# State reads kept batch by batch, and their split moved forward in block 7 of a fused attention and feed-forward kernel

## The chip, the cores and the metric

The kernel runs on one core of a Trainium2 chip. The metric is the device time of one execution in microseconds. Three runs of the kernel before took 635.97 to 636.71 us, with a median of 636.14 us.

The engines are named as the profile names them: PE is TensorE (PEld its weight loads), DVE is VectorE, ACT is ScalarE, POOL is GpSimd, and SP is the SyncE queue, from which nearly all DMA transfers are issued, one after the other.

## The reference

```python
def _attn_ref(x, state):                       # x: 8 x 8 x 512 x 64, state: 8 x 8 x 32 x 64 (batch, head, rows, width)
    scale = 1.0 / np.sqrt(D)
    scores = scale * np.matmul(x, state.transpose(0, 1, 3, 2))
    scores = scores - scores.max(-1, keepdims=True)
    a = np.exp(scores)
    a /= a.sum(-1, keepdims=True) + 1e-09
    xread = np.matmul(a, state)                # tokens read the states
    scores2 = scale * np.matmul(state, x.transpose(0, 1, 3, 2))
    scores2 = scores2 - scores2.max(-1, keepdims=True)
    a2 = np.exp(scores2)
    a2 /= a2.sum(-1, keepdims=True) + 1e-09
    sread = np.matmul(a2, x)                   # states read the tokens
    return np.concatenate([xread, sread], axis=2)

def _moe_ref(x, w_in, w_out):                  # 4352 x 512, 512 x 2048, 2048 x 512
    h = np.maximum(x @ w_in, 0.0)
    return h * h @ w_out
```

`reference` joins the heads of the attention's output to rows of 512 and feeds them through `_moe_ref`. A batch has 544 output rows: 512 of its tokens and, behind them, 32 of its states' reads.

## The kernel before, in words

The work is cut into nine blocks. Blocks 0 to 7 are the 512 token rows of the batches. Block 8 is the 256 rows of all states' reads (8 batches of 32 states), since they are too few in one batch to fill TensorE. Every product of the feed-forward part is made of three matmuls on fp32r values: each operand is split into a rounded high part and a low part that is the difference. A split is a cast (mostly on ACT) and a subtraction on DVE; `split` (L401) is the helper, and its two instructions carry the lines L410 and L404.

In a block, `hidden` steps make 16 strips of the hidden layer (`ph`), and `sum` steps multiply them with `w_out` and add into four PSUM banks x, y, z and w. From block 4 on a block's rows are taken in two halves, u = 0 and u = 1. A half has eight `sum` steps p; each needs a `parts` step, which splits the strip's values into the operands `k_hi` and `k_lo`, or `gs` (both parts in one tile). At the end of a half the banks are added up into the tiles `o_x` and `o_z` and stored (L1204 to L1222). Operands of the second half come back from DRAM as `ga` (L1097) and `gd` (L1107).

The order of all steps is a text, one word a step, that `plan` returns. `late` writes its second part, for blocks 4 to 8. A word with `~` runs a step up to its next `yield`, the bare word runs it to its end. Each engine executes its instructions in the order in which these words write them; so does SP with the transfers. In `late` the lists `a` and `z` hold what is put behind step p of the first and of the second half.

The states' reads of batches 1 to 7 are made along the way by `sread` (L742) and parked in DRAM as `sr_d`. In block 7, `move_sread` (L901) loads them back as `srn`, and splits them into the tile `sr`, which holds for each of four 128-row pieces c the high and the low part of 256 columns. Batch 0's reads come last, as `srt` of the step `sread.8`, and are split into the same tile by the same helper. `reads_by_state` (L897) says where in the 256 columns a batch stands: before, column 8 n + b for state n of batch b, so that one batch's values lie eight elements (32 bytes) apart. `hidden_reads` multiplies `sr` with the weights `s` of block 8, which `load_wi` (L917) loads back from DRAM and `split_wi` (L921) splits. `srn` and the loads of `load_wi` use the buffers of the tag `wraw`, of which there are two, so `load_wi.0` takes the buffer that `srn` leaves.

Block 8's rows of output come out in the order of the columns of `sr`, 128 at a time, on the 128 partitions of `o_x` and `o_z`. The last lines of `step_sum` (L1211 to L1223) write them to the places of the states' rows in the output. `o_x` goes in one transfer, `o_z` in two halves of its columns.

Of the kernel before, what the change touches and what calls it, by code (L numbers as in the profile page):

```python
# [144 lines left out]
def seven(blk, p, u):  # L145
    return p < FEWER[blk][u]
# [5 lines left out]
def again_order(blk):  # L152
    n = FEWER[blk][1]
    if blk == 4:
        return [2, 3, 0, 1, 4, 5, 6, 7]
    return [p + k for p in range(n - 2, -1, -2) for k in (0, 1)] + [0] * (n % 2) + list(range(n, 8))


def late():

    w = []
    for b in (4, 5, 6, 7):
        n, m, last = b + 1, b + 2, b == 7
        ob = again_order(b)
        more = {u: [""] * 8 for u in range(2)}
        a, z = more[0], more[1]
        two = f"~softmax.{n}.0 ~softmax.{n}.1"
        k = 1
        a[0] = ""
        a[k] += f" scores.{n} ~sread.{b} ~sread.{b} "  # L170
        a[1] += f" ~w2.{b}.4 w2.{b}.4 load_w2.{b}.3 "
        if last:
            a[k] += f"~exp_s.{n}.0 ~exp_s.{n}.1 sread.{b} load_n.8.0"
        else:
            a[k] += f"transposed_scores.{n}.0 transposed_scores.{n}.1 ~exp_s.{n}.0 ~exp_s.{n}.1 sread.{b} start.{m}"
        a[k + 1] += f" ~exp_s.{n}.0 ~exp_s.{n}.1 exp_s.{n}.0 exp_s.{n}.1"
        a[3] += f" ~w2.{b}.6 w2.{b}.6"
        a[3 if last else 4] += f" ~transposes.{n} ~transposes.{n} transposes.{n}"
        if last:
            a[3] += " ~move_sread"  # L180
            a[4] = "load_e.8"
            z[1] = "~move_sread move_sread load_wi.0 ~sread.8 ~sread.8 sread.8 load_wi.1"
            z[3] = "~split_wi.0 split_wi.0 load_wi.2"
            z[5] = "~split_wi.1 split_wi.1"
        else:
            a[2] += f" {two}"
            a[3] += f" {two} load_w2.{n}.0"
            a[4] += f" {two}"
            a[5] += f" {two}"
            a[6] += f" load_w2.{n}.1 {two}"  # L190
            a[7] += f" {two} ~w2.{n}.0 w2.{n}.0"
            for j, at in enumerate(XP):
                z[at] += f" load_p.{m}.{j}"
            z[2 if b > 4 else 3] += f" {two}"
            z[3] += f" ~softmax.{n}.0 softmax.{n}.0"
            z[4] += f" ~w2.{n}.2 w2.{n}.2 ~softmax.{n}.1 softmax.{n}.1 load_w2.{n}.2"
            z[5] += f" prep.{m}.0 prep.{m}.1"
            z[6] += f" prep.{m}.2 prep.{m}.3 load_e.{n} load_n.{n}.0"
        if b == 4:
            a[1] += " load_f.4"  # L200
            a[4] = a[4].replace(" transposes.5", " load_f.5 transposes.5") + " ~fewer.4"
            a[5] += " fewer.4"
            a[6] += " ~fewer.5 ~fewer.5"
            z[0] += " ~fewer.5"
            z[2] += " fewer.5"
            z[7] += " ~fewer.6 ~fewer.6"
        if b == 5:
            a[0] += " fewer.6"
        before = "accumulate.3.15" if b == 4 else f"sum.{b - 1}.1.{again_order(b - 1)[7]}"
        chain = "~hidden.{b}.{f} ~hidden.{b}.{g} {pe} ~hidden.{b}.{f} hidden.{b}.{f} {few} ~hidden.{b}.{g} {few}"  # L210
        chain += " ~parts.{b}.0.{q} hidden.{b}.{g} parts.{b}.0.{q}"

        def hide(blk, q, pe):

            if blk == 8:
                t = "~hidden.{b}.{f} ~hidden.{b}.{g} {pe} hidden.{b}.{f} {few} "
                t += f"~split_wi.{q + 1} split_wi.{q + 1} load_wi.{q + 2} " if q else ""
                t += "hidden.{b}.{g} {few} {out} {few2} parts.{b}.0.{q}"
            else:
                t = chain  # L220
            few = "~parts.{b}.0.{q}".format(b=blk, q=q) if seven(blk, q, 0) else ""
            out = f"~sum.8.0.{q - 1}" if q == FEWER[8][0] else ""
            t = t.format(b=blk, f=2 * q, g=2 * q + 1, q=q, pe=pe, out=out, few=few, few2="~parts.{b}.0.{q}".format(b=blk, q=q))
            return t

        def load(blk, at):

            return f"load_g.{blk}.{ob[at]} load_d.{blk}.{ob[at]}"

        def again(q):  # L230

            few = f"~parts.{b}.1.{q} ~parts.{b}.1.{q}" if seven(b, q, 1) else ""
            return f"{few} parts.{b}.1.{q}"

        if b == 4:
            w += [hide(4, 0, "~" + before), before, "~w2.4.2 w2.4.2 load_w2.4.2"]
        for p in range(8):
            w += [load(b, 3).split()[0]] if p == 6 else []
            if p < 7:
                w += [hide(b, p + 1, f"~sum.{b}.0.{p} " + (before if p == 0 and b > 4 else ""))]  # L240
            else:
                w += [f"~sum.{b}.0.{p}", again(ob[0])]
                w += ["sum.{}.0.{}".format(b, 6)] if FEWER[b][0] > 6 else []
            w += [f"sum.{b}.0.{p}"] if p < (6 if FEWER[b][0] > 6 else 7) else []
            w += [{4: load(b, 2), 6: load(b, 3).split()[1], 7: load(b, 4)}[p]] if p in (4, 6, 7) else []
            w += [a[p]] if p < 7 else []
        for p in range(8):
            if p == 7:
                w += [f"~hidden.{n}.0 ~hidden.{n}.1"]
            w += [f"~sum.{b}.1.{ob[p]}"]  # L250
            if p == 1:
                w += [f"sum.{b}.0.7"]
            if p < 7:
                w += [again(ob[p + 1]), f"sum.{b}.1.{ob[p]}"]
            if p == 7:
                w += [hide(n, 0, "").replace(f"~hidden.{n}.0 ~hidden.{n}.1  ", "")]
            w += [a[7]] if p == 1 else []
            w += [load(b, k) for k in {0: (5, 6), 1: (7,)}.get(p, ())]
            w += [z[p]]
    for p in range(8):  # L260
        if p < 7:
            w += [hide(8, p + 1, f"~sum.8.0.{p} " + ("sum.7.1.7" if p == 0 else ""))]
        else:
            w += ["~sum.8.0.7"]
        w += [f"sum.8.0.{p}"]
    return " ".join(w)
# [29 lines left out]
def plan():  # L296

    return " ".join([FIRST, late()])
# [3 lines left out]
def tile_attn_moe(  # L302
# [17 lines left out]
    B, H, S, D = x.shape  # L320
    Ns = state.shape[2]
    DM, DFF = w_in.shape
    P = 128
# [17 lines left out]
    traced, last = [0], {}  # L341
# [456 lines left out]
    def sets(b):  # L798

        out = {hb: 1 for hb in range(2 if "pair.0.2" in second else PART[0] // 2)} if b == 0 else {}  # L800
        while (hb := sum(out.values())) < NHB:
            out[hb] = 1 if hb % 2 else 2
        return out
# [92 lines left out]

    def reads_by_state(bs):  # L897

        return [ks[B][:, :, i].rearrange("p c (n b) -> p c b n", b=B)[:, :, bs] for i in range(2)]

    def move_sread():  # L901

        t = p2.tile([P, NC, (B - LATE) * Ns], F32, tag="wraw", name="srn", bufs=RB)
        SP.dma_start(t, sr_d)
        yield
        ks[B] = p2.tile([P, NC, 2, B * Ns], F32R, tag="w2", name="sr", bufs=WB)
        yield from split(*reads_by_state(slice(LATE, B)), t.rearrange("p c (b n) -> p c b n", n=Ns), "sr_lo")
# [247 lines left out]
    def step_sum(blk, u, p):  # L1155
        n = FEWER[blk][u]
# [21 lines left out]
        else:  # L1178
            for bank, ws in ((by, (a11, a12)), (bw, (a21, a22))):
                pairs = [(a, (wo[2 * p + k][:, 0], wo[2 * p + k][:, 1])) for k, a in enumerate(ws)]  # L1180
                if blk == B and end and bank is bw:
                    for h, half in enumerate((bw, tail := banks("acc8_0_v")[:, 0])):
                        c = ts(h, DM // 2)
                        mm3(half[:, c], [(a, [r[:, c] for r in rs]) for a, rs in pairs], first=h == 1, last=True)
                    continue
                if at == n and bank is bw:
                    for h in range(2):
                        c = ts(h, DM // 2)
# [4 lines left out]
        if at == n - 1:  # L1193
            x, z = [p2.tile([P, 2, DM // 2], F32, tag="o", name=f"o{blk}_{u}_{t}", bufs=OB) for t in "xz"]
# [14 lines left out]
                V.tensor_add(z[:, 1], bz[:, half[1]], z[:, 0])  # L1209
            held[blk, u, "o"] = x, z  # L1210
        if end:  # L1211
            n = P // B
            for i, o, bank in zip((1, 0), held.pop((blk, u, "o")), (by, bw)):
                o = o.rearrange("p h f -> p (h f)")
                halves = [slice(0, DM // 2), slice(DM // 2, DM)]
                for c in [slice(0, DM)] if blk < B or i else halves:
                    V.tensor_add(o[:, c], (tail if c.start else bank)[:, c], o[:, c])
                    if blk < B:
                        SP.dma_start(out_v[blk, ts(2 * u + i, P)], o)
                    else:  # L1220
                        rows = out_v[:, S + n * i : S + n * i + n].rearrange("b n f -> n b f")
                        SP.dma_start(rows[:, :, c], o[:, c])  # L1222

    def hidden_reads(fc):
# [30 lines left out]
    out_v = out.rearrange("(b s) f -> b s f", b=B)  # L1255
# [28 lines left out]
    ks, weights, att, accs, gs = {}, {}, {}, {}, {}  # L1284
# [132 lines left out]
    for blk in range(B + 1):  # L1417
        for hb in range(NHB):
# [11 lines left out]
            elif hb in sets(blk):  # L1430
                n = sets(blk)[hb]
# [3 lines left out]
        for fc in range(NFC):  # L1435
# [3 lines left out]
            else:  # L1439
                w = max(h for h in sets(blk) if h <= hb)  # L1440
# [33 lines left out]
    for word in plan().split():  # L1474
# [3 lines left out]
        if k not in begun:  # L1478
            f, args, after = steps[k]
# [41 lines left out]
```

## Time and profile before

| what | before |
|---|---|
| median of three runs | 636.14 us |
| the profiled execution's own time | 636.07 us |
| its span, first to last instruction | 634.2 us |
| granted TensorE clock, mean | 0.999 |
| busy: PE, DVE, ACT, POOL | 625.2, 497.3, 431.4, 26.4 us |
| DMA: bytes moved, mean rate | 109.22 MB, 172 GB/s |

The profile is of one execution. Its span is 1.9 us shorter than that execution's time, which also has what lies around the first and the last instruction. Busy times are sums of an engine's instructions; overlapping matmuls are counted once. In a timeline a row is a start, a duration and what ran; square brackets at its end give the idle time before it and what ended that. SPq is SP's queue, where a row is the issue of a transfer and not the transfer itself. A DMA share of 1.00 means that all 16 DMA engines were moving data.

### The profile page before, as it was taken

How to read it: one execution, taken by the hardware profiler on the slowest of the kernel's cores; microseconds unless marked ns; L12 is line 12 of the kernel's file. 1: busy time of each engine (PE TensorE's matmuls, PEld its weight loads, DVE VectorE, ACT ScalarE, POOL GpSimd, SP SyncE). 2: the span in 40 equal slices, each digit the busy share in tenths (PEclk: the TensorE clock that was granted, in tenths of full speed). 3: DMA queues.
4: the chain of work that ended last, by engine and by line, in shares of the span. 5: the costliest groups of instructions: out<-in, count | busy, mean ns of one | idle time of the engine just before them, and what ended most of it. 6: DMA issues, size and time to landing. Idle time of an engine off the chain costs nothing.

```text
span 634.2 us, 11622 instructions
## 1 busy us (share of the span) xinstructions
PE 625.2 (99%) x4299; PEld 519.1 (82%) x4299; DVE 497.3 (78%) x1000; ACT 431.4 (68%) x813; POOL 26.4 (4%) x37
## 2 busy tenths in 40 slices
PE   7999999999999999999999999999999999999997
PEld 6677777777787777876888898889989998999996
DVE  5989767573676888778987997999769976865996
ACT  6987658764775665778896965776567756865452
POOL 1210000000000000000000202000200020001000
PEclk9999999999999999999999999999999999999999
DMA  8983958350332776187376497747864786684321
GB/s 311 375 197 115 260 126 230 123 133 2 102 102 66 212 210 200 28 181 208 97 223 210 167 257 187 215 147 219 208 206 137 202 210 203 171 246 168 132 69 34
DMA packets 155417, 109.22 MB, mean 172 GB/s; under 512 B 104544, under 2 KB 126304, under 8 KB 155360
## 3 DMA queue, kind: packets, MB, share of 16 engines
q1 hardware_dynamic: 154544, 108.08, 59.5%
q8 instruction: 34, 0.56, 0.4%
q10 hardware_dynamic: 816, 0.39, 0.2%
q14 instruction: 23, 0.19, 0.1%
HBM read 66.83 MB, written 41.62 MB: 171 GB/s over the span
## 4 chain that ended last, share of the span: by engine, by line
PE 93%; DMA 3%; SPq 1%; ACT 1%; DVE 1%; issue 0%; ACTq 0%
PE ph L417 27%; PE acc L417 27%; PE acc_z L417 7%; PE acc_x L417 6%; PE acc_yw L417 6%; PE acc_y L417 5%; PE acc_w L417 3%; PE w2ps L429 3%; PE ph L1231 2%; PE qps L871 2%; DMA wi_raw<-in_moe_w_in_dram 2%; PE pr L748 1%; PE sc L429 1%; PE ph L1232 1%; DMA xn<-in_x_dram 1%; SPq L522 1%
## 5 line engine op out<-in xcount | busy, mean ns | idle before, releaser
L417 PE MATMUL ph<-k_hi,w 128*128 128x512 f32 x504 | 171.6, 395 | 0.0
L417 PE MATMUL acc<-wo,g_hi 128*128 128x512 f32 x512 | 159.3, 392 | 0.5 <-ACT g_hi L410 0.5
L417 PEld LDWEIGHTS ph<-k_hi,w 128*128 128x128 f32 x504 | 94.6, 188 | 29.5 <-issue 8.0
L417 PEld LDWEIGHTS acc<-wo,g_hi 128*128 128x128 f32 x512 | 95.5, 188 | 25.2 <-issue 3.6
L417 PE MATMUL acc<-wo,g_lo 128*128 128x512 f32 x256 | 99.9, 390 | 0.0
L417 PE MATMUL ph<-k_lo,w 128*128 128x512 f32 x252 | 98.3, 390 | 0.0
L1001 DVE TENSOR_TENSOR g_lo<-ph,g_hi 128x512 fp32r<-128x512 f32 x64 | 43.8, 686 | 34.6 <-ACT g_hi L410 33.7
L417 PEld LDWEIGHTS acc<-wo,g_lo 128*128 128x128 f32 x256 | 48.1, 188 | 11.2 <-DVE g_lo L1001 0.6
L993 ACT ACTIVATE ph<-ph 128x512 f32<-128x512 f32 x59 | 34.6, 586 | 30.4 <-PE ph L417 30.0
L417 PEld LDWEIGHTS ph<-k_lo,w 128*128 128x128 f32 x252 | 47.4, 188 | 8.6
L1089 ACT ACTIVATE ph<-ph 128x512 f32<-128x512 f32 x64 | 37.6, 588 | 19.5 <-PE ph L417 18.0
L994 ACT ACTIVATE ph<-ph 128x512 f32<-128x512 f32 x59 | 34.3, 582 | 1.9
L410 ACT CAST g_hi<-ph 128x512 fp32r<-128x512 f32 x53 | 31.1, 587 | 5.7 <-PE acc L417 2.8
L1141 ACT CAST k_hi<-ga 128x384 fp32r<-128x384 f32 (+1 forms) x40 | 20.9, 523 | 18.9 <-DVE ga L1240 12.8
L1146 DVE TENSOR_TENSOR k_lo<-gd,k_hi 128x512 fp32r<-128x512 f32 x36 | 24.8, 690 | 4.6 <-ACT k_hi L1145 4.6
L1198 POOL TENSOR_TENSOR o_x<-o_x 128x256 f32<-128x256 f32 x5 | 4.7, 933 | 514.1 <-ACT o_x L1196 390.6
L1090 ACT ACTIVATE ga<-ph 128x256 f32<-128x256 f32 x64 | 24.7, 386 | 2.0
L832 DVE TENSOR_TENSOR w<-w2ps,w 128x512 fp32r<-128x512 f32 (+1 forms) x34 | 20.1, 634 | 6.8 <-ACT w L410 6.8
L1145 ACT CAST gs<-gd 128x512 fp32r<-128x512 f32 x23 | 14.3, 621 | 16.3 <-DVE gd L1118 12.2
L410 ACT CAST w<-w2ps 128x512 fp32r<-128x512 f32 (+1 forms) x26 | 13.7, 568 | 17.0 <-DVE w L408 10.2
L1145 ACT CAST k_hi<-gd 128x512 fp32r<-128x512 f32 x36 | 22.4, 621 | 3.7 <-DVE gd L1118 2.8
L1141 ACT CAST gs<-ga 128x384 fp32r<-128x384 f32 (+1 forms) x32 | 17.5, 546 | 10.9 <-PE acc_yw L417 6.0
(241 smaller groups left out, 1387.1 us busy)
## 6 DMA issues: line engine op xcount, KB each, us to landing
w_d<-qo SPq DMA_DIRECT2D x32, 256.0 KB, 2.5
w2r<-w_d SPq DMA_DIRECT2D x16, 512.0 KB, 4.2
wo_raw<-in_moe_w_out_dram SPq DMA_DIRECT2D x16, 511.8 KB, 7.4
wi_raw<-in_moe_w_in_dram SPq DMA_DIRECT2D x16, 511.5 KB, 6.1
xp<-in_x_dram SPq DMA_DIRECT2D x112, 64.0 KB, 2.8
g_d<-gb SPq DMA_DIRECT2D x24, 256.0 KB, 3.0
ga<-g_d SPq DMA_DIRECT2D x24, 256.0 KB, 5.5
g_d<-ge SPq DMA_DIRECT2D x19, 256.0 KB, 2.5
```

Source lines behind the costliest of these rows:

```text
L410: A.copy(out, src)
L417: T.matmul(ps, l, r, start=first and i == 0, stop=last and i == len(seq) - 1)
L429: T.matmul(ps, l, r, start=True, stop=True)
L832: V.tensor_sub(w[:, u, g, 1], ps[g], w[:, u, g, 0].bitcast(F32))
L993: A.activation(ph, ph, AF.Relu)
L994: A.activation(ph, ph, AF.Square)
L1001: V.tensor_sub(glo, ph, ghi.bitcast(F32))
L1089: A.activation(ph, ph, AF.Relu)
L1090: A.activation(raws[blk, 0, p][:, 2 * k : 2 * k + 2].rearrange("p i t -> p (i t)"), ph[:, : 2 * P], AF.Square)
L1141: A.copy(hi[:, r], raw[:, r])
L1145: A.copy(hi[:, 4:], d)
L1146: V.tensor_sub(lo[:, 4:], d, hi[:, 4:].bitcast(F32))
```

## The change

It has three parts. The columns of `sr` are ordered batch by batch, column 32 b + n in place of 8 n + b, so that a batch's values are adjacent; the values, the matmuls and the number of instructions stay as they are. In block 7 the cast of `srn` is put at the end of the first half, and its subtraction and the load `load_wi.0` directly after the second half's first step, ahead of two other splits. And since block 8's rows now come out by batch, a last store writes 4 batches of 32 adjacent rows in place of 16 times 8 rows from eight batches.

```diff
@@ -179,7 +179,8 @@
         if last:
             a[3] += " ~move_sread"
             a[4] = "load_e.8"
-            z[1] = "~move_sread move_sread load_wi.0 ~sread.8 ~sread.8 sread.8 load_wi.1"
+            z[0] = "move_sread load_wi.0"
+            z[1] = "~sread.8 ~sread.8 sread.8 load_wi.1"
             z[3] = "~split_wi.0 split_wi.0 load_wi.2"
             z[5] = "~split_wi.1 split_wi.1"
         else:
@@ -241,6 +242,7 @@
             else:
                 w += [f"~sum.{b}.0.{p}", again(ob[0])]
                 w += ["sum.{}.0.{}".format(b, 6)] if FEWER[b][0] > 6 else []
+                w += ["~move_sread"] if last else []
             w += [f"sum.{b}.0.{p}"] if p < (6 if FEWER[b][0] > 6 else 7) else []
             w += [{4: load(b, 2), 6: load(b, 3).split()[1], 7: load(b, 4)}[p]] if p in (4, 6, 7) else []
             w += [a[p]] if p < 7 else []
@@ -896,7 +898,7 @@
 
     def reads_by_state(bs):
 
-        return [ks[B][:, :, i].rearrange("p c (n b) -> p c b n", b=B)[:, :, bs] for i in range(2)]
+        return [ks[B][:, :, i].rearrange("p c (b n) -> p c b n", b=B)[:, :, bs] for i in range(2)]
 
     def move_sread():
 
@@ -1209,7 +1211,7 @@
                 V.tensor_add(z[:, 1], bz[:, half[1]], z[:, 0])
             held[blk, u, "o"] = x, z
         if end:
-            n = P // B
+            n = P // Ns
             for i, o, bank in zip((1, 0), held.pop((blk, u, "o")), (by, bw)):
                 o = o.rearrange("p h f -> p (h f)")
                 halves = [slice(0, DM // 2), slice(DM // 2, DM)]
@@ -1218,7 +1220,7 @@
                     if blk < B:
                         SP.dma_start(out_v[blk, ts(2 * u + i, P)], o)
                     else:
-                        rows = out_v[:, S + n * i : S + n * i + n].rearrange("b n f -> n b f")
+                        rows = out_v[n * i : n * i + n, S:]
                         SP.dma_start(rows[:, :, c], o[:, c])
```

Two lines are added, so lines behind L182 stand one and those behind L243 two further down in the changed kernel. TensorE's and GpSimd's order stays. What moves on the other engines is shown at three places; a row is line, operation, out<-in and the shape of what is written.

ACT, end of block 7's first half and start of the second, before (`gs_1_6` and `k_hi_1_3` are operands of the second half):

```order
L1204 COPY o_0_x<-acc_0_x 128x256
L1141 CAST gs_1_6_6470<-ga_1_6_6340 128x384
L1145 CAST gs_1_6_6470<-gd_1_6_6358 128x512
L1141 CAST k_hi_1_3_6508<-ga_1_3_6298 128x384
L1145 CAST k_hi_1_3_6508<-gd_1_3_6300 128x512
L410 CAST sr<-srn 128x4x7x32
```

The same place in the changed kernel:

```order
L1206 COPY o_0_x<-acc_0_x 128x256
L412 CAST sr<-srn 128x4x224
L1143 CAST gs_1_6_6472<-ga_1_6_6340 128x384
L1147 CAST gs_1_6_6472<-gd_1_6_6358 128x512
L1143 CAST k_hi_1_3_6513<-ga_1_3_6298 128x384
L1147 CAST k_hi_1_3_6513<-gd_1_3_6300 128x512
```

The cast of the reads moved ahead of four casts, and what it writes is 4 runs of 224 in place of 4 x 7 x 32 single elements.

DVE, start of the second half, before:

```order
L1142 TENSOR_TENSOR gs_1_6_6470<-ga_1_6_6340,gs_1_6_6470 128x384
L1146 TENSOR_TENSOR gs_1_6_6470<-gd_1_6_6358,gs_1_6_6470 128x512
L1217 TENSOR_TENSOR o_0_x<-acc_0_y,o_0_x 128x512
L1217 TENSOR_TENSOR o_0_z<-acc_0_w,o_0_z 128x512
L1142 TENSOR_TENSOR k_lo_1_3_6509<-ga_1_3_6298,k_hi_1_3_6508 128x384
L1146 TENSOR_TENSOR k_lo_1_3_6509<-gd_1_3_6300,k_hi_1_3_6508 128x512
L404 TENSOR_TENSOR sr<-srn,sr 128x4x7x32
```

In the changed kernel:

```order
L1144 TENSOR_TENSOR gs_1_6_6472<-ga_1_6_6340,gs_1_6_6472 128x384
L1148 TENSOR_TENSOR gs_1_6_6472<-gd_1_6_6358,gs_1_6_6472 128x512
L406 TENSOR_TENSOR sr<-srn,sr 128x4x224
L1219 TENSOR_TENSOR o_0_x<-acc_0_y,o_0_x 128x512
L1219 TENSOR_TENSOR o_0_z<-acc_0_w,o_0_z 128x512
L1144 TENSOR_TENSOR k_lo_1_3_6514<-ga_1_3_6298,k_hi_1_3_6513 128x384
L1148 TENSOR_TENSOR k_lo_1_3_6514<-gd_1_3_6300,k_hi_1_3_6513 128x512
```

The reads' subtraction moved ahead of the two output additions and the two `k_lo` subtractions.

SP's queue, the same stretch and then its end, before (`o_0` is the output of block 7's first half, at the end that of block 8):

```order
L1107 DMA gd_1_0_6481<-g_d_104 128x512
L1219 DMA out_dram<-o_0_x 128x512
L1219 DMA out_dram<-o_0_z 128x512
L1097 DMA ga_1_7_6514<-g_d_111 128x512
L919 DMA wi_0_6519<-wi_d_98 128x4x256
```

```order
L919 DMA wi_5_6940<-wi_d_100 128x4x256
L919 DMA wi_6_7002<-wi_d_101 128x4x256
L919 DMA wi_7_7064<-wi_d_101 128x4x256
L1222 DMA out_dram<-o_0_x 16x8x512
L1222 DMA out_dram<-o_0_z 16x8x256 x2
```

In the changed kernel:

```order
L1109 DMA gd_1_0_6483<-g_d_104 128x512
L921 DMA wi_0_6486<-wi_d_98 128x4x256
L1221 DMA out_dram<-o_0_x 128x512
L1221 DMA out_dram<-o_0_z 128x512
L1099 DMA ga_1_7_6519<-g_d_111 128x512
```

```order
L921 DMA wi_5_6940<-wi_d_100 128x4x256
L921 DMA wi_6_7002<-wi_d_101 128x4x256
L921 DMA wi_7_7064<-wi_d_101 128x4x256
L1224 DMA out_dram<-o_0_x 4x32x512
L1224 DMA out_dram<-o_0_z 4x32x256 x2
```

The first load of block 8's weights moved ahead of two stores and a load, and the destination of the last three stores changed from 16 x 8 rows to 4 x 32 rows.

## Rows read from the trace of the kernel before

**Rows 1.** The page's busy times: us, share of the span, instructions.

```profile
PE 625.2 (99%) x4299; PEld 519.1 (82%) x4299; DVE 497.3 (78%) x1000; ACT 431.4 (68%) x813; POOL 26.4 (4%) x37
```

**Rows 2.** What PE waited for from 50 to 626: us in total, times, longest.

```profile
PE acc L417 <- ACT g_hi L410: 0.5, 1, 0.5
```

**Rows 3.** Busy time by stretch: us, PE, PEld, DVE, ACT, POOL, PEclk, DMA share, GB/s.

```profile
570.00:580.00 10.00, 10.00 (x141) 9.78 (x140) 6.94 (x11) 6.10 (x13) 0.00 (x0) 1.00 0.66 229
...
630.00:634.20 4.20, 0.00 (x1) 0.00 (x0) 0.42 (x1) 0.00 (x0) 0.00 (x0) 0.84 0.44 125
```

**Rows 4.** Timeline of ACT, 563 to 583 us: start, duration, what.

```profile
563.38 0.38 ACT L1204 COPY o_x<-acc_x 128x256 f32<-128x256 f32 x1
565.92 0.51 ACT L1141 CAST gs<-ga 128x384 fp32r<-128x384 f32 x1 [2.16 <-PE acc_w L417]
...
567.80 1.97 ACT L410 CAST sr<-srn 128x896 fp32r<-128x896 f32 x1
...
582.09 0.62 ACT L1141 CAST gs<-ga 128x512 fp32r<-128x512 f32 x1 [1.56 <-PE acc_yw L417]
```

**Rows 5.** Timeline of DVE, 566 to 572 us.

```profile
566.99 0.69 DVE L1146 TENSOR_TENSOR gs<-gd,gs 128x512 fp32r<-128x512 f32 x1
567.60 0.68 DVE L1217 TENSOR_TENSOR o_x<-acc_y,o_x 128x512 f32<-128x512 f32 x1
...
569.26 0.69 DVE L1146 TENSOR_TENSOR k_lo<-gd,k_hi 128x512 fp32r<-128x512 f32 x1
569.86 1.90 DVE L404 TENSOR_TENSOR sr<-srn,sr 128x896 fp32r<-128x896 f32 x1
```

**Rows 6.** Timeline of PE, 572 to 573 us, two products that read `k_lo`.

```profile
572.18 0.28 PE L417 MATMUL acc_x<-wo,k_lo 128*128 128x256 f32 x1
...
572.89 0.28 PE L417 MATMUL acc_z<-fewer,k_lo 128*128 128x256 f32 x1
```

**Rows 7.** Timeline of SP's queue, 554 to 580 us: issues of transfers.

```profile
554.96 0.78 SPq L904 DMA_DIRECT2D srn<-sr_d  x1
...
568.31 0.34 SPq L1219 DMA_DIRECT2D out_dram<-o_x  x1
...
569.37 0.40 SPq L1097 DMA_DIRECT2D ga<-g_d  x1
571.79 7.71 SPq L919 DMA_DIRECT2D wi<-wi_d  x3
```

**Rows 8.** Tile `s`: ns min/median/max, first and last start, shapes.

```profile
L1231 PE MATMUL ph<-sr,s x64: 389/395/403, 584.4 to 624.0; 128*128 128x512 f32 x64
...
L410 ACT CAST s<-wi x8: 1049/1052/1054, 576.6 to 618.2; 128x1024 fp32r<-128x1024 f32 x8
L404 DVE TENSOR_TENSOR s<-wi,s x8: 1217/1218/1224, 577.7 to 619.5; 128x1024 fp32r<-128x1024 f32 x8
```

**Rows 9.** Tile `out_dram`, issue times of stores: ns min/median/max, first and last start.

```profile
L1219 SPq DMA_DIRECT2D out_dram<-o_z x8: 337/338/338, 377.3 to 592.1; - x8
L1222 SPq DMA_DIRECT2D out_dram<-o_z x2: 554/568/581, 630.1 to 630.8; - x2
L1222 SPq DMA_DIRECT2D out_dram<-o_x x1: 616/616/616, 629.4 to 629.4; - x1
```

**Rows 10.** Busy time by short stretch; the last two columns are DMA share and GB/s.

```profile
592.60:593.00 0.40, 0.40 (x5) 0.40 (x4) 0.36 (x2) 0.34 (x2) 0.00 (x0) 1.00 0.99 369
...
630.60:631.20 0.60, 0.00 (x0) 0.00 (x0) 0.00 (x0) 0.00 (x0) 0.00 (x0) 1.00 0.88 171
...
631.60:632.20 0.60, 0.00 (x0) 0.00 (x0) 0.00 (x0) 0.00 (x0) 0.00 (x0) 1.00 0.87 304
...
632.70:634.20 1.50, 0.00 (x0) 0.00 (x0) 0.00 (x0) 0.00 (x0) 0.00 (x0) 0.56 0.03 10
```

**Rows 11.** What SP waited for from 560 to 634, at its last line.

```profile
SPq L1516 <- DMA out_dram<-o_x: 1.0, 1, 1.0
```

**Rows 12.** DMA rate from 566 to 575 us in 40 equal slices.

```profile
GB/s 237 373 373 237 228 264 310 282 246 273 364 328 200 237 164 155 127 146 146 173 264 310 337 337 391 401 401 410 391 392 382 419 291 287 319 355 396 360 350 300
```

## The prediction

> **What bounds the kernel now.** I read the page's busy times first [rows 1]: TensorE is busy for 625.2 of 634.2 us, so work of another engine is worth something only where TensorE waits for it. Second, the list of what TensorE waited for between 50 and 626 us [rows 2]: it has one entry, 0.5 us. Third, the busy times by stretch [rows 3]: TensorE is busy for 10.00 of 10 us from 570 to 580, at full granted clock, and for 0.00 of the last 4.2 us. So the program is one unbroken TensorE chain and then a tail of 4.2 us that holds nothing but the last addition and the last stores. The reader should carry away two places: block 7's second half (565 to 585 us), in which most of the edit lies and in which time is hidden behind TensorE, and the tail after 630 us, in which nothing hides anything. Fourth, I read the timelines of ACT, DVE, TensorE and SP around 563 to 585 us [rows 4 to 7], and fifth the DMA engines' load by stretch at the end [rows 10].
>
> **The cast and the subtraction of the reads.** Their size stays 896 elements a partition; what changes is that they write runs of 224 instead of single elements 32 bytes apart. Now they take 1.97 us on ACT [rows 4] and 1.90 us on DVE [rows 5]. The nearest contiguous rows are the splits of `s`, 1.052 and 1.218 us for 1024 elements [rows 8]; times 896/1024 that makes an estimated 0.92 and 1.07 us, a saving of 1.05 us on ACT and 0.83 us on DVE. The other end is that nothing is saved. I take the contiguous price, since size and types are those of the `s` rows. The last state's small pair of casts shrinks likewise by a few tenths.
>
> *ACT.* The cast now stands right behind the copy of `acc_x` that ends at 563.76 us, ahead of the `gs` cast that starts at 565.92 after 2.16 us idle [rows 4]. Its input's load was issued at 554.96 [rows 7]. At 0.92 us it ends near 564.7, at the old 1.97 us at 565.75: both fit the idle stretch, so ACT's next cast is not late. Cost 0.
>
> *DVE.* The subtraction now stands behind the `gs` subtraction that starts at 566.99 and takes 0.69 us. It runs from about 567.60 (where the `o_x` addition now starts) to 568.67, or to 569.50 at the old price. Behind it two output additions and the two `k_lo` subtractions move back by its length: the second of these ends now at 569.95 [rows 5], 2.35 us after the `o_x` addition starts, and then at about 571.0, or 571.85 at the old price; the first ends some 0.6 us before it. TensorE reads the first one's result at 572.18 and the second one's at 572.89 [rows 6]. That is a slack of 1.8 us, 0.9 at the old price. Cost 0, hidden by TensorE's own products, which stand in line before them. From 571 on DVE is earlier than now.
>
> *SP.* The load `wi_0` goes ahead of two output stores and one `ga` load. It needs the buffer that the subtraction frees; now it issues at 571.79, right at that subtraction's end [rows 5, 7]. It would issue at about 568.7, and SP stands waiting for it for most of the microsecond before. What is queued behind it: the stores of `o_x` (now 568.31) and `o_z`, and the `ga` load (569.37) [rows 7], each about 1 us later, the stores also because their additions are. The `ga` load feeds the last product of the half, whose cast starts at 582.09 [rows 4]; the stores free buffers that the second half's output takes after that. Both have more than 8 us. The split of `wi_0` can start earlier, but its first reader on TensorE starts at 584.4 us [rows 8]. So this load gains nothing that the end sees, and costs nothing.
>
> Sum of the middle: 0, with a bound of about 0.1 us on either side, since TensorE has no gap there to give back and no new wait.
>
> **The last three stores.** Only these lie on the path that sets the end. The bytes stay: 256 KB of `o_x` and two halves of 128 KB of `o_z`, 128 rows in SBUF. The destination changes from 16 steps of 8 rows, a batch's rows apart, to 4 steps of 32 adjacent rows. When SP ends the program it waits for their landing, 1.0 us for that of `o_x` alone [rows 11]: nothing runs beside them.
>
> Now data begin to move near 630.6 us and have moved by 632.7 us, 2.1 us for 524,288 bytes [rows 10]. What the new pattern does depends on how a transfer is dealt to the 16 DMA engines. If by the outermost step of the destination, 4 engines do the work of 16. The price of that comes from what one engine delivers: in 592.6 to 593.0 us, with block 7's last plain stores in flight (the latest issued at 592.1 [rows 9]), 369 GB/s at a share of 0.99, or 23.3 GB/s an engine; in 631.6 to 632.2 us, mostly 1 KB pieces of the halves, 304 GB/s at 0.87, or 21.8 GB/s [rows 10]. So `o_x` takes 262,144 / (4 x 23.3) = 2.81 us and the halves 262,144 / (4 x 21.8) = 3.01 us; the queue is behind from the first byte, so they follow each other: 5.8 us in place of 2.1, **3.7 us more**. If the deal is by SBUF partitions, of which there are 128 as before, it costs 0.
>
> No transfer of the kernel before shows an outermost count under 16, so these two are the ends. I take the first. The issue times speak for it: a plain 128-row store is issued in 0.338 us, these stores of the same or half the bytes in 0.568 to 0.616 us [rows 9]. So the queue works on the destination's steps as they are written and does not flatten them to 128 rows first; and the store of now has just the 16 outer steps that keep 16 engines at a share of 0.88 [rows 10].
>
> The Trainium skill has a rule for it that speaks against this change ("DMA: Bandwidth & Descriptors", section "Why a DMA increments its semaphore by 16 and not by 1"): a transfer issued from SP uses the largest number of engines up to 16 that divides both patterns' slowest dimension. By it these stores run on 4 engines, which is the sum above; without it the sum is 0. No row here shows it.
>
> Bounds of the dear end. Fast: the best slice of the middle moved 419 GB/s [rows 12], 26.2 GB/s an engine; 524,288 / (4 x 26.2) = 5.0 us, 2.9 more. Slow: while `o_x` moves now, the engines give 171 GB/s at 0.88, 12.1 GB/s each [rows 10]; with that for `o_x` (5.4 us) and 3.0 for the halves it is 8.4 us, 6.3 more. I expect less, since adjacent rows replace rows a batch apart, and four engines press on the memory less than 16.
>
> **Sum.** 0 + 3.7 us. The profiled execution took 636.07 us, its span 634.2; the median of the runs is 636.14, so nothing has to be corrected, and I add to that: 639.8 us, 0.6% more. A measurement of this kernel can tell about 0.2% from no change, which is 1.3 us.
>
> **Rivals.**
> 1. *The stores stay on 16 engines* (the deal goes by SBUF partitions, or the pieces are dealt out singly). Not slower, then: the tail is as now, 636.1 us. The issue might fall from 0.57 toward 0.34 us each, which brings the last data at most 0.4 us forward; or rise by 0.1 each. 635.7 to 636.4. For it: the SBUF side does keep 128 rows, and no row here shows an unequal deal. Against it: the issue times above. It decides from the point where the stores move over 200 GB/s in the tail, more than four engines give by any row above.
> 2. *TensorE waits in block 7.* The moved subtraction stands ahead of the two `k_lo` subtractions. It costs from the point where it ends later than 570.4 us, so that the first `k_lo` (1.75 us behind it) misses 572.18 [rows 6]. That needs its input or its cast nearly 2 us late, which neither ACT's idle stretch nor the load's issue at 554.96 suggests [rows 4, 7]. A subtraction that ends 1 us past that point makes 637.1 us with the stores as now.
> 3. *Four engines, and each as slow as in the first 0.6 us of the tail throughout*: 524,288 / (4 x 12.1) = 10.8 us, 8.7 more, 644.8 us. Against it: plain stores run at nearly twice that an engine.
>
> **How the numbers follow.** Four engines at 2.8 to 6.3 us more: 0.80. Four engines outside that, rival 3 with it: 0.02. Sixteen engines: 0.15. Rival 2 or something else in the middle: 0.03. The forecast is the first, 639.8 us; its bounds are 638.9 and 642.4 us, which hold 8 in 10 by themselves, so the range stops there and leaves out the case of 16 engines. Slower by over 0.2%: 0.83, the two four-engine cases and a third of the last. Faster by over 0.2% would need 1.3 us out of a tail whose data alone take 2.1 us, or a gap of TensorE that is not there: 0.02. The rest, 0.15, is no change.
>
> **What would show it.** In the profile after: TensorE busy without a gap from 560 to 630 us and its end at the same time within 0.2 us; the cast near 0.92 us inside ACT's old idle stretch; the subtraction near 1.07 us starting at 567.6; `wi_0` issued near 568.7. In the tail a DMA share near 0.25 at some 90 GB/s for 5 to 6 us instead of up to 0.9 at 170 to 300 GB/s, and the landing of the last half about 3.7 us later. The forecast is wrong if the tail's DMA share still comes near 0.9, or if the four engines are there and the end comes less than 2.8 us later, which would mean that an engine alone is faster than any slice of this trace shows.

## Result and profile after

The changed kernel takes **641.84 us** (median of 6 runs, 640.71 to 641.96); the kernel before took 637.2 us in the same sessions (6 runs, 635.97 to 638.14). The ratio is 1.0078 with a 95% interval of 1.0064 to 1.0092: slower by 4.1 to 5.9 us. The forecast was 639.8 us in a range of 638.9 to 642.4.

The profiled execution took 641.84 us with a span of 640.0. The page's busy times and, in the second fence, what TensorE waited for from 50 us to the end (us in total, times, longest):

```profile
PE 626.0 (98%) x4299; PEld 519.8 (81%) x4299; DVE 495.7 (77%) x1000; ACT 430.2 (67%) x813; POOL 26.3 (4%) x37
```

```profile
PE acc L419 <- ACT g_hi L412: 0.5, 1, 0.5
PE qps L873 <- ACT qo L877: 0.4, 1, 0.4
```

Busy time by stretch (us, PE, PEld, DVE, ACT, POOL, PEclk, DMA share, GB/s):

```profile
560.00:570.00 10.00, 10.00 (x73) 9.41 (x72) 6.51 (x13) 6.99 (x15) 0.00 (x0) 1.00 0.84 278
570.00:580.00 10.00, 10.00 (x140) 9.78 (x139) 7.80 (x14) 5.51 (x12) 0.00 (x0) 1.00 0.77 251
...
630.40:631.00 0.60, 0.19 (x2) 0.00 (x0) 0.37 (x1) 0.00 (x0) 0.00 (x0) 1.00 0.00 0
631.00:632.00 1.00, 0.00 (x0) 0.00 (x0) 0.06 (x1) 0.00 (x0) 0.00 (x0) 1.00 0.22 25
632.00:633.00 1.00, 0.00 (x0) 0.00 (x0) 0.00 (x0) 0.00 (x0) 0.00 (x0) 1.00 0.21 18
633.00:634.00 1.00, 0.00 (x0) 0.00 (x0) 0.00 (x0) 0.00 (x0) 0.00 (x0) 1.00 0.23 63
634.00:635.00 1.00, 0.00 (x0) 0.00 (x0) 0.00 (x0) 0.00 (x0) 0.00 (x0) 0.78 0.27 98
...
636.00:637.00 1.00, 0.00 (x0) 0.00 (x0) 0.00 (x0) 0.00 (x0) 0.00 (x0) 0.50 0.27 97
...
638.00:640.00 2.00, 0.00 (x0) 0.00 (x0) 0.00 (x0) 0.00 (x0) 0.00 (x0) 0.50 0.05 17
```

Block 7 is as unbroken as before: TensorE is busy for 10.00 of 10 us from 560 to 570 and from 570 to 580, the latter as in [rows 3]. Its last product ends at 630.59 us (0.19 us into the window from 630.40), and it is idle for the remaining 9.4 us. Before, it ended at 630.0 with a tail of 4.2 us [rows 3]. So the tail grew by 5.2 us. In the tail the DMA share is 0.21 to 0.27 where it was 0.87 to 0.88 [rows 10], and the rate is 18 to 98 GB/s where it was 171 to 304.

The other 0.6 us of the profiled difference lies ahead of the tail and does not belong to the change. One of the early output stores, long before the first moved instruction, already goes out at 215.2 us (L1267) where it went at 214.3 (L1265 before). In the profiles of all kernels of this study, with the moves and without, TensorE ends between 629.4 and 630.8 us; two of those that lack the moves end at 630.0 (before) and 630.8 (order only, below). The medians differ by 4.6 us, and their interval holds the 5.2 us of the tail.

The moved instructions. ACT from 563.9 us (start, duration, what, idle before in brackets):

```profile
563.99 0.38 ACT L1206 COPY o_x<-acc_x 128x256 f32<-128x256 f32 x1
564.25 0.95 ACT L412 CAST sr<-srn 128x896 fp32r<-128x896 f32 x1
566.53 0.51 ACT L1143 CAST gs<-ga 128x384 fp32r<-128x384 f32 x1 [1.33 <-PE acc_w L419]
```

DVE from 567.6 us:

```profile
567.60 0.69 DVE L1148 TENSOR_TENSOR gs<-gd,gs 128x512 fp32r<-128x512 f32 x1
568.21 1.08 DVE L406 TENSOR_TENSOR sr<-srn,sr 128x896 fp32r<-128x896 f32 x1
569.21 0.68 DVE L1219 TENSOR_TENSOR o_x<-acc_y,o_x 128x512 f32<-128x512 f32 x1
...
570.87 0.68 DVE L1148 TENSOR_TENSOR k_lo<-gd,k_hi 128x512 fp32r<-128x512 f32 x1
```

SP's queue from 568 us:

```profile
569.32 0.60 SPq L921 DMA_DIRECT2D wi<-wi_d  x1
570.01 0.57 SPq L1221 DMA_DIRECT2D out_dram<-o_x  x1
...
571.15 0.45 SPq L1099 DMA_DIRECT2D ga<-g_d  x1
```

The whole profile is 0.6 us later here than that of before, so 0.6 is taken off in comparisons. The cast takes 0.95 us in place of 1.97 [rows 4] and lies in ACT's old idle stretch, of which 1.33 us are left. The subtraction takes 1.08 in place of 1.90 [rows 5]. The load `wi_0` leaves at 569.32, right behind the subtraction's end. The second `k_lo` subtraction ends at 571.55, 1.0 us later than before [rows 5] once the 0.6 is taken off, and nothing waits for it.

What SP waited for at its last line (us in total, times, longest), then the DMA view from 629 to 640 us (busy tenths and GB/s in 40 slices of 0.275 us, then the packets by size):

```profile
SPq L1518 <- DMA out_dram<-o_x: 3.9, 1, 3.9
SPq L1518 <- DMA out_dram<-o_z: 2.6, 2, 1.3
```

```profile
DMA  0000000025050122222222222222222221100000
GB/s 0 0 0 0 0 0 0 0 52 37 0 22 0 15 52 67 52 82 97 89 97 89 108 97 101 89 97 97 93 101 93 101 74 56 48 0 0 0 0 0
DMA packets 396, 0.52 MB, mean 48 GB/s; under 512 B 12, under 2 KB 268, under 8 KB 396
```

SP's wait for `o_x` grew from 1.0 [rows 11] to 3.9 us, and the wait for the halves that follows grew from 0.8 to 2.6 us. Data run from 631.2 to 638.6 us (first and last slice that is not 0): 7.4 us in place of 2.1. Two things are to be seen. From 634 on the rate stands near 96 GB/s. In the three windows before that, 631 to 634, only 25 + 18 + 63 = 106 KB moved, at a share that is hardly lower: the engines are in use, but slow.

### The profile page after: what moved, and what is told of

It reads as the page before. It is cut to its first block, busy times and chain, and to the rows that moved or that the text cites. A ratio compares the mean times of both kernels' runs of the same rounds, so it can differ in the third digit from the quotient of the medians.

```text
span 640.0 us, 11621 instructions
## 1 busy us (share of the span) xinstructions
PE 626.0 (98%) x4299; PEld 519.8 (81%) x4299; DVE 495.7 (77%) x1000; ACT 430.2 (67%) x813; POOL 26.3 (4%) x37
## 4 chain that ended last, share of the span: by engine, by line
PE 93%; DMA 2%; ACT 2%; SPq 1%; issue 0%; DVE 0%; ACTq 0%
PE ph L419 27%; PE acc L419 26%; PE acc_yw L419 7%; PE acc_z L419 7%; PE acc_x L419 7%; PE acc_y L419 5%; PE acc_w L419 3%; PE w2ps L431 3%; PE ph L1233 2%; PE qps L873 2%; PE pr L750 1%; PE sc L431 1%; PE ph L1234 1%; DMA wi_raw<-in_moe_w_in_dram 1%; PE ph L976 1%; SPq L524 1%
## 5 line engine op out<-in xcount | busy, mean ns | idle before, releaser
L549 DVE STREAM_TRANSPOSE xT<-xp 128x512 f32<-128x512 f32 x28 | 18.8, 693 | 8.0 <-DMA xp<-in_x_dram 8.0
```

## Experiments

Main theory: the steps of the destination's outermost dimension are dealt out to the DMA engines, so four steps give four engines, and nothing else of the change is seen in the time. Rivals: the moves cost something; the pace follows from the rows' places in memory rather than from the way the steps are dealt out.

**The moves alone.** The changed kernel with the old columns and the old stores.

```diff
-        return [ks[B][:, :, i].rearrange("p c (b n) -> p c b n", b=B)[:, :, bs] for i in range(2)]
+        return [ks[B][:, :, i].rearrange("p c (n b) -> p c b n", b=B)[:, :, bs] for i in range(2)]
...
-            n = P // Ns
+            n = P // B
...
-                        rows = out_v[n * i : n * i + n, S:]
+                        rows = out_v[:, S + n * i : S + n * i + n].rearrange("b n f -> n b f")
```

> Moves alone: the cast, the subtraction and the load stand where the change puts them, the columns of sr and the last stores are those of the kernel before. Engine theory (the 5.2 us come from the last stores, whose destination has 4 outermost steps and so 4 DMA engines): the tail from TensorE's last product to the end of the span is 4.2 us as before, DMA share in it up to about 0.9, and the time equals the kernel before's within 0.2%. Cast and subtraction keep their old prices, 1.97 and 1.90 us, and still nothing waits on TensorE. Rival, block 7: if the moves delay TensorE, the time is above the kernel before's by up to the 5 us seen.

Measured: 636.79 us (12 runs) against 637.09, ratio 0.9992 (0.9978 to 1.0005): no difference. Tile `sr` (ns min/median/max, first and last start, shapes) and SP's wait at the end:

```profile
L412 ACT CAST sr<-srn x1: 2008/2008/2008, 563.8 to 563.8; 128x896 fp32r<-128x896 f32 x1
L406 DVE TENSOR_TENSOR sr<-srn,sr x1: 1967/1967/1967, 567.8 to 567.8; 128x896 fp32r<-128x896 f32 x1
```

```profile
SPq L1518 <- DMA out_dram<-o_x: 1.0, 1, 1.0
```

Even at the old price, 2.01 and 1.97 us, the moved pair stays hidden, and the tail is that of before (4.2 us). Rival 2 of the prediction falls.

**The order alone.** The kernel before with the new columns and the new stores, without the moves.

```diff
-        return [ks[B][:, :, i].rearrange("p c (n b) -> p c b n", b=B)[:, :, bs] for i in range(2)]
+        return [ks[B][:, :, i].rearrange("p c (b n) -> p c b n", b=B)[:, :, bs] for i in range(2)]
...
-            n = P // B
+            n = P // Ns
...
-                        rows = out_v[:, S + n * i : S + n * i + n].rearrange("b n f -> n b f")
+                        rows = out_v[n * i : n * i + n, S:]
```

> Order alone: columns by batch and the last stores of 4 x 32 rows, the cast, subtraction and load where the kernel before has them. Engine theory: the whole loss is here, ratio to the kernel before 1.006 to 1.009, tail about 9.4 us at a DMA share near 0.25. The cast takes about 0.95 and the subtraction 1.08 us in the old place. Rival, block 7: no loss, ratio within 1.002. It also shows whether the slow first 1.8 us of the tail (18 to 25 GB/s) come again.

Measured: 642.03 us (6 runs), ratio 1.0078 (1.0062 to 1.0094), the same as the whole change. The DMA view from 629 to 640 us shows the same slow start and the same plateau:

```profile
GB/s 0 0 0 0 0 0 0 0 7 52 30 0 22 7 30 45 67 67 82 89 97 97 97 101 89 101 97 97 97 97 93 101 89 71 48 37 0 0 0 0
```

SP's waits at the end are 3.9 and 2.6 us, those of the changed kernel to the digit. The whole loss comes with this part.

**Same rows, other order of the steps.** The changed kernel with the destination's two outer dimensions swapped: 32 steps of 4 rows that cover the same 128 rows. Each row of `o_x` and `o_z` then lands in another of these 128 places, so this kernel is for timing the stores alone.

```diff
-                        rows = out_v[n * i : n * i + n, S:]
+                        rows = out_v[n * i : n * i + n, S:].rearrange("b n f -> n b f")
```

> The changed kernel, but a last store walks its 128 rows as 32 outer steps of 4 (state, then batch) in place of 4 of 32. Each store writes the same 128 places of the output, with rows at other ones of them than the reference. Engine theory: 32 outermost steps give 16 engines, the tail is 4.2 to 4.6 us at a share up to 0.9, the time within 0.2% of the kernel before. Rival, memory: if writing these rows of four batches is slow in itself, the tail stays near 9.4 us and the ratio near 1.008.

Measured: 636.34 us (12 runs), ratio 0.9988 (0.9973 to 1.0002). The same view:

```profile
DMA  0000000079992940000000000000000000000000
GB/s 0 0 0 0 0 0 0 0 290 372 358 346 82 320 138 0 0 0 0 0 0 0 0 0 30 0 0 0 0 0 0 0 0 0 0 0 0 0 0 0
DMA packets 433, 0.53 MB, mean 48 GB/s; under 512 B 48, under 2 KB 304, under 8 KB 432
```

With the same bytes from the same partitions to the same rows, the share reaches 0.9 again, and the data are through in 1.9 us. Only the order in which the destination's steps are written differs. So it is this order, with its outermost count, that sets the number of engines, not the SBUF side and not the rows; the count itself is varied in the next run. The tail is 3.8 us, 0.4 shorter than before the change.

**Eight steps.** Columns in two halves of 16 states, in each batch by batch, so that a store writes 8 batches of 16 rows; each split becomes two instructions.

```diff
+        return [[ks[B][:, :, i, 128 * h : 128 * h + 128].rearrange("p c (b n) -> p c b n", b=B)[:, :, bs] for i in range(2)] for h in range(2)]
...
+            n = P // B
...
+                        rows = out_v[:, S + n * i : S + n * i + n]
```

> Dose: columns by half of the states, then batch, then state, so that a last store writes 8 outermost steps of 16 adjacent rows; cast and subtraction come as two instructions each. Engine theory: 8 engines, DMA share near 0.5 at about 180 GB/s, 524288 / (8 x 22.5) = 2.9 us of data in place of 2.1, the tail 5.0 us if the start is not slow, up to 6 if it is; ratio 1.001 to 1.003. Rival, memory (adjacent rows are slow): nearer to 9 us than to 5. Rival, SBUF deal: 4.2 us.

Measured: 637.6 us (12 runs), ratio 1.0009 (0.9997 to 1.0021); tail 6.1 us.

```profile
DMA  0000662435455555420000001000000000000000
GB/s 0 0 0 15 104 45 22 52 104 179 179 197 183 197 186 194 171 78 0 0 0 0 0 0 30 0 0 0 0 0 0 0 0 0 0 0 0 0 0 0
DMA packets 409, 0.53 MB, mean 48 GB/s; under 512 B 24, under 2 KB 280, under 8 KB 408
```

The plateau lies near 186 GB/s at a share of 0.5: eight engines at 23 GB/s each, the pace of the four. The tail grew by 1.9 us, while the runs show 1.3 us at most. Its TensorE ended early in the profile, at 629.4; what of this is the edit and what the spread between executions isn't settled.

**Other places in memory.** Four adjacent-row groups lie 544 rows apart in the output. Two kernels write the last three stores to a scratch buffer instead, with groups 544 and 552 rows apart, and leave the reads' rows of the output unwritten. The edit for 544:

```diff
-                        rows = out_v[n * i : n * i + n, S:]
+                        rows = sd[n * i : n * i + n, 512 : 512 + Ns]
...
+    sd = tc.dram_tile([B, 544, DM], F32, name="sd")
```

> The changed kernel, but its last three stores write the same pattern (4 outer steps, 544 rows apart, of 32 adjacent rows) to a scratch tensor in DRAM; the output's 256 rows of the reads are left out. Control for the next run. If the slow start of the tail belongs to the pattern, it comes again here: some 25 and 18 GB/s in the first two us, share near 0.25 throughout, tail near 9.4 us. If it belongs to the output tensor, the start is fast, the tail about 7.6 to 7.9 us.

> As the run before with outer steps 552 rows apart in place of 544, so that the four engines, each at the same row of its own batch, are no longer a multiple of 64 KB from each other. Lockstep theory (the four engines hit the same part of the memory until they have drifted apart): the start is fast, near 95 GB/s from the first half us, tail 7.6 to 7.9 us. Few-engine theory (four engines start slowly whatever the addresses): same as the control, near 9.4 us. Share near 0.25 in both.

Measured: 641.14 and 641.96 us (one run each), tails of 9.3 us both. SP's wait for `o_x` at the end and the rate from 629 to 640 us, 552 rows (the 60 in the first slice is not of these stores):

```profile
SPq L1519 <- DMA sd<-o_x: 4.0, 1, 4.0
GB/s 60 0 0 0 0 0 0 0 22 60 7 15 7 7 30 67 60 60 89 97 89 97 108 97 93 97 93 101 93 97 93 101 89 67 45 26 0 0 0 0
```

The wait stays as in the changed kernel, and so does the slow start. Neither the distance between the groups nor the output buffer is its cause.

**One such store by itself.** The kernel before with two extra stores of 256 KB and 4 x 32 rows to scratch, in block 8, issued 5.3 us apart, with no other transfer near.

```diff
+        if blk == B and p in (5, 6):
+            t = hi.bitcast(F32)[:, 4:].rearrange("p i t -> p (i t)")
+            SP.dma_start(probe[p - 5][:, :Ns], t)
...
+    probe = [tc.dram_tile([4, Ns + 1, DM], F32, name=f"probe{i}") for i in range(2)]
```

> The kernel before, with two more stores of 256 KB to scratch in DRAM, each of 4 outer steps of 32 adjacent rows, alone on the DMA engines at about 617 and 623 us (they read the split operand of block 8's products 5 and 6). Both are done before the last stores, so the time is that of the kernel before. Few-engine theory (such a store starts slowly by itself): each shows the slow first 1.5 us, 4 to 4.5 us from first to last byte. Queue theory (the slow start comes from the next two stores being dealt to the same four engines while the first still runs): 2.8 us each at about 95 GB/s from the first half us on.

Measured: 636.52 us (one run) against 636.47; the extra stores are hidden. Busy time by stretch, columns as above:

```profile
619.10:620.10 1.00, 1.00 (x9) 0.93 (x8) 0.93 (x4) 0.94 (x2) 0.00 (x0) 1.00 0.21 25
620.10:621.10 1.00, 1.00 (x11) 1.00 (x10) 1.00 (x2) 0.06 (x1) 0.00 (x0) 1.00 0.18 12
621.10:622.10 1.00, 1.00 (x11) 1.00 (x10) 0.93 (x4) 0.00 (x0) 0.00 (x0) 1.00 0.24 74
622.10:623.00 0.90, 0.90 (x7) 0.78 (x6) 0.86 (x4) 0.59 (x2) 0.00 (x0) 1.00 0.26 100
...
624.00:625.00 1.00, 1.00 (x8) 0.86 (x7) 0.97 (x3) 0.06 (x1) 0.00 (x0) 1.00 0.06 14
625.00:626.00 1.00, 1.00 (x11) 1.00 (x10) 0.52 (x3) 0.55 (x2) 0.00 (x0) 1.00 0.30 18
626.00:627.00 1.00, 1.00 (x11) 1.00 (x10) 0.72 (x2) 0.73 (x2) 0.00 (x0) 1.00 0.18 47
627.00:628.00 1.00, 1.00 (x8) 0.73 (x8) 0.88 (x2) 0.09 (x1) 0.00 (x0) 1.00 0.25 98
```

The first store had nothing behind it or beside it, and still moved at 25 and 12 GB/s in its first two windows and at 74 in the next before it reached 100; the second did much the same. So the slow start belongs to each such store when its queue is empty, and stores queued behind it don't cause it.

**Both wishes at once.** Columns by groups of 4 batches, in each state by state, then batch: a store writes 32 steps of 4 rows, the destination of the third experiment, with columns to match it. The moves are kept; the cast and the subtraction of `srn` become two instructions each, writing single elements 16 bytes apart.

```diff
+                to = [ks[B][:, :, i, P * g : P * g + P].rearrange("p c (n b) -> p c b n", b=4)[:, :, u - 4 * g : v - 4 * g] for i in range(2)]
...
-                        rows = out_v[n * i : n * i + n, S:]
+                        rows = out_v[n * i : n * i + n, S:].rearrange("b n f -> n b f")
```

> A version with 16 engines and rows of four batches a store: columns by group of four batches, then state, then batch, so that a last store has 32 outer steps of 4 rows, at the right places. Cast and subtraction come as two instructions each, writing elements 16 bytes apart. Engine theory: tail as in the 32-step run, 3.8 us or less (4.2 in the kernel before), ratio 0.998 to 1.000; the data of the last stores move at over 340 GB/s from the start. Cast and subtraction together between the contiguous 0.95 and 1.08 us and the old 1.97 and 1.90 us; nothing of that is seen at the end. If 16 bytes apart is as dear as 32, the old sums come again.

Measured: 635.34 us (12 runs) against 637.07, ratio **0.9975** (0.9963 to 0.9987): 0.25% faster than the kernel before, and faster than the changed one. Tail 3.7 us in place of 4.2. Tile `sr`:

```profile
L412 ACT CAST sr<-srn x2: 890/1016/1142, 563.4 to 564.1; 128x384 fp32r<-128x384 f32 x1, 128x512 fp32r<-128x512 f32 x1
L910 DVE TENSOR_TENSOR sr<-srn,sr x2: 875/992/1109, 567.4 to 568.2; 128x384 fp32r<-128x384 f32 x1, 128x512 fp32r<-128x512 f32 x1
```

The casts take 0.89 + 1.14 = 2.03 us and the subtractions 1.98: nothing is saved there, and nothing lost, because both are hidden.

**The same with a second queue.** The first half of `o_z` is stored from ACT's queue.

```diff
-                        SP.dma_start(rows[:, :, c], o[:, c])
+                        (A if c.stop < DM else SP).dma_start(rows[:, :, c], o[:, c])
```

> As the run before, with the first half of o_z stored from the queue of ACT, which is idle by then, so that the issue of the second half on SP does not wait for it. If the tail is bound by issue, the second half is issued near its addition's end instead of 0.3 us later and the tail falls by 0.2 to 0.3 us to some 3.5 us; if it is bound by the data or by the landing alone, it stays at 3.8 us. The time stays within 0.1% of the run before either way.

Measured: 635.18 us (12 runs), ratio 0.9977 (0.9963 to 0.9991); tail 3.7 us, the same to a tenth as without it, and not the 0.2 to 0.3 shorter that a bound by the issues would give. The issues on one queue do not bound the tail.

**Without the moves.** The kernel of "Both wishes at once" with the old order in block 7.

```diff
-            z[0] = "move_sread load_wi.0"
-            z[1] = "~sread.8 ~sread.8 sread.8 load_wi.1"
+            z[1] = "~move_sread move_sread load_wi.0 ~sread.8 ~sread.8 sread.8 load_wi.1"
...
-                w += ["~move_sread"] if last else []
```

> The quads' columns and 32-step stores, with cast, subtraction and load where the kernel before has them. If the moves in block 7 are worth nothing, tail and time are those of the quads with the moves: tail 3.7 us, ratio 0.997 to 0.9995. If the moves carry part of the gain, the ratio is nearer to 1 by more than the interval.

Measured: 635.97 us (11 runs) against 636.47, ratio 0.9991 (0.9977 to 1.0005); tail 3.8 us. The interval meets that of the version with the moves at 0.9977 to 0.9987. The tail explains 0.4 to 0.5 us of the gain, some 0.07%; whether the rest of that version's 0.25% is the moves or the spread between executions stays open. The moves alone, above, made no difference that can be told.

## Why the prediction was right, and what was mis-sized

**The middle: right, 0.** The cast was estimated at 0.92 us and took 0.95, the subtraction at 1.07 and took 1.08. `wi_0` left where it was expected, 568.7 plus the profile's offset of 0.6. TensorE has no gap in block 7, and the order alone costs what the whole change costs. One sign was not met: TensorE ends at 630.6 us, not within 0.2 of 630.0; that is the offset above, which was there by 215 us.

**Four engines: right.** The trace of the kernel before could not show it, and the prediction rested on an inference. Two readings bear it out. The plateau is 97 to 98 GB/s in the windows from 634 and 636 us, 24 GB/s for each of four engines; forecast were 21.8 and 23.3. And the DMA view counts packets under 512 bytes: 48 before the change and with 32 steps, 24 with eight, 12 with four, for three stores in each kernel. That is 16, 8 and 4 for a store, one for each engine if the reading is right. The rule of the Trainium skill ("DMA: Bandwidth & Descriptors", section "Why a DMA increments its semaphore by 16 and not by 1"), that a transfer takes the largest number of engines up to 16 that divides both patterns' slowest dimensions, agrees with all four patterns: 4, 8, 16 and 32 steps against 128 partitions.

One argument for it was weak, though. The prediction read the issue times of 0.57 to 0.62 us [rows 9] as a sign that the destination's steps are used as written. With 32 steps of 4 rows, on 16 engines, the issues take 0.55 to 0.59 us: such a time tells a three-dimensional destination from a plain one, not the number of engines.

**The size: the step that failed is the term "5.8 us in place of 2.1" for the data of the last stores.** They took 7.4 us, so the term is 5.3 and not 3.7 us, and the tail grew by 5.2. The rate of a running engine was right; 524,288 bytes at 96 GB/s are 5.5 us. What was missing is the start: the 106 KB that moved between 631.2 and 634 would take 1.1 us at 96 GB/s and took 2.8, a loss of 1.7 us. The last slices, at 74, 56 and 48 GB/s, make the remaining 0.2 to 0.3.

The row that hinted at this was there: in the first 0.6 us in which data moved before the change an engine gave 12.1 GB/s [rows 10]. The prediction made it the slow bound, for the whole of `o_x`, and then chose the fast price with the sentence that adjacent rows should do better than rows a batch apart, and four engines better than 16. Both reasons fail, and two more readings of the kernel before say why. The first fence is its tail from 629 to 634.2 us (40 slices of 0.13 us); the second is two short stretches in which block 7's plain stores, issued at 591.51 and 592.10 us, begin to move (columns as above).

```profile
GB/s 0 0 0 0 0 0 0 0 0 0 0 0 95 236 126 221 126 189 331 354 386 355 355 189 197 189 213 299 150 24 0 0 0 0 0 0 0 0 0 0
DMA packets 432, 0.52 MB, mean 101 GB/s; under 512 B 48, under 2 KB 304, under 8 KB 432
```

```profile
591.90:592.30 0.40, 0.40 (x4) 0.35 (x3) 0.40 (x2) 0.40 (x2) 0.00 (x0) 1.00 0.00 0
592.30:592.60 0.30, 0.30 (x3) 0.26 (x2) 0.27 (x2) 0.30 (x1) 0.00 (x0) 1.00 0.86 321
```

The old pattern, 16 steps of 8 rows, also starts slowly: six slices, 0.8 us, at a mean of 165 GB/s, before it passes 330. The 32 steps of 4 run on 16 engines too (48 small packets in both) and, like the old 8, lie a batch apart, yet they start at 290 and 372 GB/s. So few engines are not needed for a slow start. Nor are adjacent rows its cause by themselves: a plain store writes 128 adjacent rows as 128 steps of one, and the two above come out of an idle stretch at 321 GB/s and then 369 [rows 10]. What goes with the start in all five patterns is the number of rows in one step: with 1 and 4 it is not slow, with 8 it is for 0.8 us, with 16 for some 1.4 us and with 32 for 2.8 us. Whether the rows of a step are themselves the cause, and by what, the traces do not show.

**The rivals.** Sixteen engines: the decision point of 200 GB/s was never reached (108 at most). A wait in block 7: fell with the moves alone. Four engines at 12.1 GB/s each throughout: wrong for the plateau, and for the first 2 us even too kind (25 and 18 GB/s in place of 4 x 12.1).

The result lies in the range because the slow bound was kept in it: the tail grew by 5.2 us, between the forecast 3.7 and the 6.3 of that bound. The distance of the median from the forecast, 2.0 us, overstates the miss. The sum starts from 636.14 us, the median of three runs, and six runs of that kernel beside the result have 637.2; 1.1 us are this base. By the medians the change costs 4.6 us, 0.9 more than forecast. The lower bound of 2.8 us is 2.9 by its own sum, which changes nothing.

## What to carry to other kernels

Before a store's rows are reordered, look at how many steps the outermost dimension of its DRAM side has: with four instead of 16 the last stores took 7.4 us in place of 2.1, where nothing could hide them. The same rows written as 32 steps of 4 were through in 1.9 us, and the kernel whose columns match that order was no slower than the one before (635.34 against 637.07 us). Look also at the rows of one step: with 16 engines at work, 8 rows a step still started slower than 4. And casts and subtractions that halve in a stretch where TensorE has no gap are worth 0: the time for such an edit is decided by its side effects at the unhidden end.

## What the runs showed of the hardware

- A store from SBUF whose destination has many rows in one outer step starts slowly, with its engines in use. With four steps of 32 rows it moves at 12 to 25 GB/s in the first two windows of a microsecond (share 0.18 to 0.22); with eight steps of 16 at 22 to 104 GB/s for some 1.4 us; with 16 steps of 8 at a mean of 165 GB/s for 0.8 us; with 32 steps of 4 not at all (290 GB/s in the first slice). The first showed in another buffer, with other distances between the groups, and in a store with no other transfer near. What the engines do in that time the traces don't show; its cause stays open.
- An element of 4 bytes written every 16 bytes cost as much as one every 32: 2.03 us (in two instructions) and 2.01 for the cast, 1.98 and 1.97 for the subtraction, where adjacent elements took 0.95 and 1.08.
